# Linear attention and a gated MLP in one kernel: attention in blocks of 64 tokens on four quarters of the array

## The chip, the cores and the metric

One NeuronCore of one Trainium2 chip runs the whole program. The metric is the device time of one execution in microseconds (us), inputs already in HBM. The profile is one execution taken by the hardware profiler. "TensorE" is PE in the rows (PEld: its weight loads), VectorE DVE, ScalarE ACT, GpSimd POOL, SyncE's queue SP.

## The reference

Inputs: q, k, v of 4 sequences x 8 heads x 768 tokens x 64, a decay `lam` per head, MLP weights 512x1536 (gate, value) and 1536x512 (out), a norm weight. All fp32.

```
for each block of 64 tokens:
    intra = (q_b k_b^T * Dmask) v_b            # Dmask[i,j] = lam^(i-j) for i>=j, else 0
    inter = (q_b * lam^(i+1)) kv_state
    out_b = intra + inter
    kv_state = lam^block * kv_state + (k_b * lam^(block-1-j))^T v_b
x   = attention out as 3072 rows of 512
xn  = x / sqrt(mean(x^2) + 1e-6) * rms_g
out = (silu(xn w_gate) * (xn w_val)) w_out
```

The result does not depend on the block's length except for rounding.

## The kernel before

Tokens come in six groups of 512 (`G`), heads in four pairs, so there are 24 pieces of attention, called pairs here (class `Pair`, L457). A pair's q, k, v are loaded in fp32 (`load_qkv`, L92): q and k with the 64 dimensions of two heads along the partitions, k and v again with tokens along them. The attention works in blocks of 128 tokens, four to a group. Its steps per pair, with the lines of their matmuls:

- `scores` (L468, matmul L477): k q^T of each block and head, 64 rows of the array by 128 columns, 128 moving columns; the two heads use the two row halves and write two banks.
- `decay_a` (L489) multiplies them by a mask of powers on VectorE (L497); `decay_k` (L482) scales k on ScalarE; `decay_q` (L499) scales q by the powers `pw` on GpSimd (L501).
- `state_sums` (L503, matmul L510): k^T v of each block, full height by 64 columns, two heads in the two column halves. A sequence's last block needs none.
- `states` (L515): the running state, on VectorE: a copy for a sequence's first block (L523), else state x power + sum (L525).
- `mix_chunks` (L530, matmul L538): masked scores times v; `mix_states` (L543, matmul L549): state times scaled q, 64x64 on the two diagonal quarters, both heads into the one bank `po`. A sequence's first block has no state.
- `keep_output`, `keep_squares` (ScalarE) take the bank away for the norm.

The powers are made in the opening by scans on VectorE (`powers`, L150: 8 masks L153 and 4 rows `pw` L158).

The MLP runs in fp16 with each operand split in a high and a low part, in three products: groups 0 and 1 classically (L668), groups 2 to 5 by a scheme with seven products of quarter blocks (L779); the last layer likewise (L938 for group 0, L1050). Weights are converted from fp32 bits on the chip during groups 0 and 1. Attention of group 0 and part of group 1 fills the opening, before there is an fp16 operand; the rest lies between the MLP's steps.

PSUM has eight banks: four of pool `ps_g` (MLP, and the odd pairs of group 0), two of `ps_s` (scores; for groups 3 to 5 sums and `po` too), two of `ps_o` (`oa`, `ob`: sums and `po` of groups 0 to 2, results of the last layer).

The order of the work on every engine is fixed when the program is built. `Plan` (L1089) holds steps with an engine, a cost, a due time and the tiles that they read, write and open; `Plan.run` (L1154) simulates the engines and takes the steps by due time. `SHIFTS` (L1760) moves single steps' due times. `Plan.shared` (L1150) names the steps of VectorE that GpSimd must not overlap: a GpSimd step after one of them waits for it. `TURN` (L1143) is the planner's charge for going from fp16 work to attention steps and back. Engines then wait on each other by semaphores, each in its own order.

## Time and profile before

| | |
|---|---|
| three timed runs | 630.33, 631.5, 631.6 us; median 631.5 |
| the profiled execution's own time | a span of 628.2 us from its first to its last instruction; what lies around the span is not in the trace |
| TensorE busy | 622.2 us, 99% |
| VectorE, ScalarE, GpSimd busy | 452.8, 383.9, 127.6 us |
| moved by DMA | 144.05 MB, mean 229 GB/s |

Busy time of an engine is the union of its instructions. A matmul's end is modelled: its record lasts longer than the array is taken by it, so spacing of starts, not the length of one, shows what a matmul costs. Rows give the line, engine, operation, output and inputs by the program's names (`pa` scores, `pst` sums, `po` mix), shapes and counts.

### The profile page before, as it was taken

The numbers are of one execution on the slowest core, as the hardware profiler recorded it, in microseconds if no ns is written. First come the engines' busy times: TensorE is split into PE (matmuls) and PEld (weight loads), VectorE is DVE, ScalarE is ACT, GpSimd is POOL, SyncE is SP. The second block draws the span as 40 slices with busy tenths as digits, with TensorE's granted clock in tenths as the row PEclk, the third lists the DMA queues.
The fourth block names the chain that finished last, engine by engine and source line by source line (L and its number), as shares of the span: only waits on it lengthen the run. The fifth ranks groups of instructions, "written<-read, shape, count | busy, mean of one in ns | idle before, by whom it ended". The sixth has DMA issues, their size and how long they took to land.

```text
span 628.2 us, 14174 instructions
## 1 busy us (share of the span) xinstructions
PE 622.2 (99%) x5665; PEld 479.3 (76%) x5665; DVE 452.8 (72%) x886; ACT 383.9 (61%) x724; POOL 127.6 (20%) x113
## 2 busy tenths in 40 slices
PE   9999999999999999999999999999999999999997
PEld 8864444455657777668888888888889888888886
DVE  6889888777787778788875789634874778546641
ACT  3779799986546764568764685534853564445531
POOL 3531201142825665410020110011000110000000
DMA  8899898888646788878878667744675667343401
GB/s 320 305 318 299 313 313 290 288 279 290 231 148 226 258 284 273 275 265 284 269 268 297 216 212 225 244 179 152 226 224 179 202 207 248 109 135 105 148 18 51
DMA packets 56033, 144.05 MB, mean 229 GB/s; under 512 B 5920, under 2 KB 18208, under 8 KB 54560
## 3 DMA queue, kind: packets, MB, share of 16 engines
q1 hardware_dynamic: 55824, 142.64, 67.3%
q8 instruction: 44, 0.72, 0.5%
q10 hardware_dynamic: 144, 0.52, 0.3%
q14 instruction: 21, 0.17, 0.1%
HBM read 106.96 MB, written 36.18 MB: 228 GB/s over the span
## 4 chain that ended last, share of the span: by engine, by line
PE 94%; DMA 2%; DVE 1%; ACT 1%; SPq 0%; issue 0%; POOL 0%; ACTq 0%; POOLq 0%
PE o L1050 20%; PE pa L779 20%; PE pb L779 15%; PE pv L668 9%; PE pg L668 9%; PE o L938 5%; PE pa L477 4%; PE po L538 3%; PE po L549 3%; DMA qkv<-in_qkv_dram 2%; PE o_own L1050 2%; PE pst L510 2%; PE pss L589 1%; PE unread L144 1%; PE pr L630 0%
## 5 line engine op out<-in xcount | busy, mean ns | idle before, releaser
L779 PEld LDWEIGHTS <-gw 128*128 128x128 f16 x1440 | 139.5, 98 | 21.9 <-issue 0.8
L1050 PE MATMUL o<-wo,late 128*128 128x256 f16 x1152 | 143.9, 273 | 0.5 <-ACT late L1061 0.5
L1050 PEld LDWEIGHTS <-late 128*128 128x128 f16 x1260 | 123.0, 98 | 15.1 <-issue 0.8
L668 PEld LDWEIGHTS <-w_half 128*128 128x128 f16 x576 | 53.9, 98 | 60.5 <-issue 1.5
L833 ACT COPY tx<-pa 128x256 f32<-128x256 f32 x96 | 35.3, 371 | 72.9 <-PE pa L779 55.5
L779 PE MATMUL pa<-tx,gw 128*128 128x256 f16 x576 | 77.4, 273 | 0.0
L668 PE MATMUL pv<-x,w_half 128*128 128x512 f16 x288 | 69.2, 379 | 0.2
L668 PE MATMUL pg<-x,w_half 128*128 128x512 f16 x288 | 66.8, 379 | 0.0
L837 DVE TENSOR_TENSOR tx<-pb,tx 128x256 f32<-128x256 f32 x96 | 40.0, 420 | 31.4 <-PE pb L779 29.1
L779 PEld LDWEIGHTS <-gv 128*128 128x128 f16 x576 | 56.0, 98 | 7.4 <-issue 0.2
L501 POOL TENSOR_TENSOR qkv<-qkv,pw 128x512 f32<-128x512 f32 x24 | 30.6, 1275 | 74.8 <-PE pa L477 66.5
L845 DVE TENSOR_TENSOR sg<-pb,sg 128x256 f32<-128x256 f32 x48 | 20.1, 422 | 35.4 <-ACT sg L841 30.7
L1013 DVE TENSOR_TENSOR late<-s,late 128x1024 f16<-128x1024 f32 x30 | 37.3, 1253 | 5.2 <-ACT late L1009 5.1
L708 POOL TENSOR_TENSOR r<-w_half 128x512 f32<-128x512 f16 x24 | 27.7, 1163 | 63.3 <-DVE w_half L440 25.5
L497 DVE TENSOR_TENSOR a<-pa,mask 128x512 f32<-128x512 f32 x48 | 31.4, 683 | 12.0 <-PE pa L477 8.5
L779 PE MATMUL pa<-x,gv 128*128 128x256 f16 x288 | 39.3, 273 | 0.0
L779 PE MATMUL pb<-x,gv 128*128 128x256 f16 x288 | 39.3, 273 | 0.0
L779 PE MATMUL pa<-x,gw 128*128 128x256 f16 x288 | 39.0, 273 | 0.0
L779 PE MATMUL pb<-tx,gw 128*128 128x256 f16 x288 | 39.0, 273 | 0.0
L779 PE MATMUL pb<-x,gw 128*128 128x256 f16 x288 | 38.7, 273 | 0.0
L938 PE MATMUL o<-wo,early 128*128 128x512 f16 x144 | 34.9, 379 | 0.0
L729 POOL TENSOR_TENSOR ws<-ws,ws 128x512 f16<-128x512 f32 x24 | 28.8, 1210 | 29.3 <-DVE en L325 15.3
(152 smaller groups left out, 1031.0 us busy)
## 6 DMA issues: line engine op xcount, KB each, us to landing
gw<-gw_kept SPq DMA_DIRECT2D x48, 640.0 KB, 4.8
qkv<-in_qkv_dram SPq DMA_DIRECT2D x47, 512.0 KB, 6.0
h<-h_kept SPq DMA_DIRECT2D x30, 512.0 KB, 4.1
h_kept<-sg SPq DMA_DIRECT2D x48, 256.0 KB, 3.4
gv<-gw_kept SPq DMA_DIRECT2D x48, 256.0 KB, 4.4
raw_gv<-in_weights_dram SPq DMA_DIRECT2D x11, 1024.0 KB, 7.2
raw_o<-in_weights_dram SPq DMA_DIRECT2D x24, 256.0 KB, 4.4
gw_kept<-ws SPq DMA_DIRECT2D x12, 512.0 KB, 4.2
```

Source lines behind the costliest of these rows:

```text
L477: nc.tensor.matmul(self.pa[j][:, c, :], self.kT[r, c, :], self.qT[r, c, :], start=True, stop=True,)
L497: nc.vector.tensor_mul(self.a[:, j], self.pa[j], decay)
L501: eng.tensor_mul(self.qT, self.qT, pw[:, p : p + 1, :].broadcast_to([P, GC, P]))
L668: nc.tensor.matmul(ps, w[:, kk, :], x[:, kk, :], start=i == kk == 0, stop=i == 2 and kk == NK - 1,)
L708: nc.gpsimd.tensor_add(self.r[:, i], w[:, 0], w[:, 1])
L729: eng.tensor_sub(self.to[:, c, 1], self.t[:, c], self.to[:, c, 0])
L779: nc.tensor.matmul(ps, w(ow, k), x(ox, k), start=first and i == k == 0, stop=i == 2 and k == 1, skip_group_check=True,)
L833: nc.scalar.copy(self.val_sums[:, self.half(t)], self.pa)
L837: nc.vector.tensor_add(v, self.pb, v)
L938: nc.tensor.matmul(self.banks[t], h[:, oh, t * P : (t + 1) * P], wo[:, j, 3 + 2 * k : 5 + 2 * k, ow], start=j == k == i == 0, stop=j == HA ...
L1013: eng.tensor_sub(lo, of, hi)
L1050: nc.tensor.matmul(bank[:, t], ops[:, oh, t * P : (t + 1) * P], w[:, ow], start=n in (1, 2, 5) and q == i == 0 and (t == 0 or bank is own) ...
```

## The change

Attention goes in blocks of 64 tokens, the reference's own. A group is now 256 tokens of two sequences (groups 0 to 2: sequences 0 and 1; 3 to 5: sequences 2 and 3), in place of 512 tokens of one; the host lays out q, k, v so and `send` writes the rows accordingly. Every attention matmul has 64 rows, 64 columns and 64 moving columns, and the loops go round the four 64x64 quarters of the array. Both heads, and both sequences with their heads crossed, lie so that the two row halves write different banks or different partitions.

- Scores: 16 matmuls a pair; sums 16, into the second half of the scores' two banks, so that one buffer `s` of two banks holds both; `decay_a` covers 512 elements a partition in place of 1024.
- States: one step for each of a group's four blocks, with an update for each of the two sequences; a sequence's first state is copied on ScalarE.
- The mix is two halves, `mix_others` and `mix_states` (which begins with the second half of the mix and goes on with the states), 8 + 8 + 16 matmuls. Between them stands a fence: a memset of one column on GpSimd (`between`) that waits for the first half's last matmul, and for which the second half's first matmul waits. Both halves add to the same places from different row halves.
- `po` of groups 0 to 2 and the last layer's results share one buffer `oo` of two banks; `po` of groups 3 to 5 takes the buffer `s`.
- Masks are three scans of 64 a pair on VectorE; all `pw` are made on GpSimd by one copy and six products (`powers_of_pairs`). The row of zeros and its ScalarE instruction (L204, L205) go.
- The planner's costs follow, and the table `SHIFTS` is new: 2726 entries in place of 856.

```diff
-ps_s = ctx.enter_context(tc.tile_pool(name="ps_s", bufs=2, space=PSUM))
+ps_s = ctx.enter_context(tc.tile_pool(name="ps_s", bufs=1, space=PSUM))
...
-lam_b, lam_p, gcol = cs[:, :H], cs[:, H : H + NP], cs[:, H + NP :]
+lam_b, lam_p, gcol = cs[:, :H], cs[:, H : H + 2 * NP], cs[:, H + 2 * NP :]
...
-SLOTS = GC + 1
+LAST = S // D - 1
...
-state = const.tile([P, NP, SLOTS, D], F32, name="state")
-mask = const.tile([P, H, P], F32, name="mask")
-pw = const.tile([P, NP, P], F32, name="pw")
-def powers(p, part):
-    if part < 2:
-        h = 2 * p + part
-        nc.vector.tensor_tensor_scan(
-            mask[:, h, :], lam_b[:, h : h + 1].broadcast_to([P, P]), ident, 0.0,
-            ALU.mult, ALU.add,
+state = const.tile([P, NP, 2, 2, D], F32, name="state")
+mask = const.tile([P, NP, 3, D], F32, name="mask")
+pw = const.tile([P, NP, 2, 1, D], F32, name="pw")
+diag = const.tile([P, D], F32, name="diag")
+nc.gpsimd.tensor_add(diag, ident[:, :D], ident[:, D:])
+def powers(p, n):
+    h = 2 * p + n % 2
+    nc.vector.tensor_tensor_scan(
+        mask[:, p, n], lam_b[:, h : h + 1].broadcast_to([P, D]), diag, 0.0, ALU.mult, ALU.add,
+    )
+def powers_of_pairs():
+    to = pw.rearrange("p n q o i -> p (n q) (o i)")
+    lam = lam_p.rearrange("p (n i) -> p n i", i=1)
+    nc.gpsimd.tensor_copy(to[:, :, :1], lam)
+    n = 1
+    while n < D:
+        nc.gpsimd.tensor_mul(
+            to[:, :, n : 2 * n], to[:, :, :n],
+            to[:, :, n - 1 : n].broadcast_to([P, 2 * NP, n]),
         )
-    else:
-        nc.vector.tensor_tensor_scan(
-            pw[:, p, :], lam_p[:, p : p + 1].broadcast_to([P, P]), zeros, 1.0,
-            ALU.mult, ALU.add,
-        )
+        n *= 2
...
+fence = const.tile([P, 1], F32, name="fence")
+def after(instruction, name, reason="row tiles"):
+    tc.add_manual_dep(
+        instruction, name,
+        mybir.DependencyInfo(mybir.DependencyClass.Sync, mybir.DependencyReason.DATA), reason=reason,
+    )
...
-        self.scores_room, self.scores_tag = (ps_g, "g") if self.turn else (ps_s, "s")
+        self.scores_tag = "g" if self.turn else "s"
+        self.mix_tag = "oo" if self.early else "s"
     qT, kT, k, v = (property(lambda s, i=i: loaded[s.m, s.p][i]) for i in range(4))
-    def scores(self, chunks=range(GC)):
+    def block(self, c, s):
+        return (self.m % 3) * GC + (c % 2) * 2 + s, c // 2
+    def scores(self):
         m, p = self.m, self.p
-        if 0 in chunks:
-            self.pa = [
-                self.scores_room.tile([P, GC, P], F32, tag=self.scores_tag, name=f"pa_{m}_{p}_{j}")
-                for j in range(2)
+        if self.turn:
+            self.pa = None
+            self.banks = [
+                ps_g.tile([P, G], F32, tag="g", name=f"pa_{m}_{p}_{j}") for j in range(2)
             ]
-        for c in chunks:
-            for j, r in enumerate(heads):
-                nc.tensor.matmul(
-                    self.pa[j][:, c, :], self.kT[r, c, :], self.qT[r, c, :],
-                    start=True, stop=True,
-                )
+        else:
+            self.pa = ps_s.tile([P, 2, G], F32, tag="s", name=f"pa_{m}_{p}")
+            self.banks = [self.pa[:, j] for j in range(2)]
+        for c, q, s, row in itertools.product(range(2), repeat=4):
+            b, half, r = 2 * q + c, slice(s * D, (s + 1) * D), heads[row]
+            nc.tensor.matmul(
+                self.scored(row)[half, c, q], self.kT[r, b, half], self.qT[r, b, half],
+                start=True, stop=True, skip_group_check=True,
+            )
+    def scored(self, row):
+        return self.banks[row][:, : GC * D].rearrange("p (c q i) -> p c q i", c=2, q=2)
...
     def decay_a(self, part=None):
         p = self.p
         if not part:
-            self.a = att.tile([P, 2, GC, P], F32, tag="a", name=f"a_{self.m}_{p}")
-        for j in range(2):
-            if part in (None, j):
-                h = 2 * p + j
-                decay = mask[:, h : h + 1, :].broadcast_to([P, GC, P])
-                nc.vector.tensor_mul(self.a[:, j], self.pa[j], decay)
+            a = att.tile([P, (2 * GC + 2 * (GC - 1)) * D], F32, tag="a", name=f"a_{self.m}_{p}")
+            self.a = a[:, : 2 * GC * D].rearrange("p (r c x) -> p r c x", r=2, c=2)
+            self.inner = a[:, 2 * GC * D :].rearrange("p (q t d) -> p q t d", q=2, d=D)
+        for row in range(2) if part is None else (part,):
+            decay = mask[:, p : p + 1, row : row + 2].rearrange("p n q i -> p n (q i)")
+            nc.vector.tensor_mul(
+                self.a[:, row], self.scored(row).rearrange("p c q i -> p c (q i)"),
+                decay.broadcast_to([P, 2, 2 * D]),
+            )
     def decay_q(self, eng=nc.gpsimd):
+        q = self.qT.rearrange("p (q c) (s i) -> p q (c s) i", q=2, s=2)
+        eng.tensor_mul(q, q, pw[:, self.p].broadcast_to([P, 2, GC, D]))
+    def sum_of(self, c, s):
+        return self.banks[s][:, (GC + c) * D : (GC + c + 1) * D]
+    def state_sums(self):
+        for c in range(GC):
+            for s in range(2):
+                t, q = self.block(c, s)
+                if t == LAST:
+                    continue
+                half = slice(s * D, (s + 1) * D)
+                for j, r in enumerate(heads):
+                    nc.tensor.matmul(
+                        self.sum_of(c, s)[heads[j ^ q]], self.k[half, c, r], self.v[half, c, r],
+                        start=True, stop=True, skip_group_check=True,
+                    )
+    def state(self, t):
+        if t % GC == GC - 1:
+            return state[:, self.p, :, t // GC % 2]
+        return self.inner[:, :, t % GC]
+    def first_states(self):
+        sums = self.banks[0][:, GC * D : 2 * GC * D].rearrange("p (q x) -> p q x", q=2)
+        nc.scalar.copy(self.state(0), sums[:, :, :D])
+    def states(self, t):
         p = self.p
-        eng.tensor_mul(self.qT, self.qT, pw[:, p : p + 1, :].broadcast_to([P, GC, P]))
-    def state_sums(self):
-        m, p = self.m, self.p
-        pool, tag = (ps_o, "oa") if self.early else (ps_s, "s")
-        self.pst = pool.tile([P, GC, P], F32, tag=tag, name=f"pst_{m}_{p}")[:, :, :D]
-        for c in range(GC):
-            if (m * GC + c) % SEQ_CH < SEQ_CH - 1:
-                for r in heads:
-                    nc.tensor.matmul(
-                        self.pst[r, c, :], self.k[:, c, r], self.v[:, c, r],
-                        start=True, stop=True,
-                    )
-    def states(self, chunks=range(GC)):
-        m, p = self.m, self.p
-        for c in chunks:
-            g = m * GC + c
-            if g % SEQ_CH == SEQ_CH - 1:
-                continue
-            new = state[:, p, g % SLOTS, :]
-            if g % SEQ_CH == 0:
-                nc.vector.tensor_copy(new, self.pst[:, c, :])
-            else:
+        for c, s in [(c, s) for s in range(2) for c in range(GC)]:
+            at, q = self.block(c, s)
+            if at == t:
+                new, old = (self.state(x)[:, q] for x in (t, t - 1))
                 nc.vector.scalar_tensor_tensor(
-                    new, state[:, p, (g - 1) % SLOTS, :], pw[:, p, P - 1 : P],
-                    self.pst[:, c, :], ALU.mult, ALU.add,
+                    new, old, pw[:, p, q, 0, D - 1 : D], self.sum_of(c, s), ALU.mult, ALU.add,
                 )
-    def mix_chunks(self, chunks=range(GC)):
-        m, p = self.m, self.p
-        if 0 in chunks:
-            pool, tag = (ps_g, "g") if self.turn else (ps_o, "ob") if self.early else (ps_s, "s")
-            self.po = pool.tile([P, GC, P], F32, tag=tag, name=f"po_{m}_{p}")
-        po = self.po
-        for c in chunks:
-            for j, r in enumerate(heads):
+    def mix(self, other):
+        for c, q, j in itertools.product(range(2), repeat=3):
+            s = j ^ q ^ other
+            half = slice(s * D, (s + 1) * D)
+            a = self.a[half, j ^ q, c, q * D : (q + 1) * D]
+            nc.tensor.matmul(
+                self.po[heads[j], q, 2 * c + s], self.v[half, 2 * q + c, heads[j]], a,
+                start=bool(other) and c == 0, stop=False, skip_group_check=True,
+            )
+            if not (other or c or q or j):
+                after(traced[-1], self.fence)
+        self.last = traced[-1].name
+    def mix_others(self):
+        pool = ps_o if self.early else ps_s
+        po = pool.tile([P, 2, G], F32, tag=self.mix_tag, name=f"po_{self.m}_{self.p}")
+        self.po = po[:, :, : GC * D].rearrange("p q (b i) -> p q b i", b=GC)
+        self.mix(1)
+    def between(self):
+        nc.gpsimd.memset(fence, 0.0)
+        after(traced[-1], self.last)
+        self.fence = traced[-1].name
+    def mix_states(self):
+        self.mix(0)
+        for b, q, j in itertools.product(range(GC), range(2), range(2)):
+            t = self.m % 3 * GC + b
+            if t:
+                r = heads[j ^ q]
                 nc.tensor.matmul(
-                    po[r, c, :], self.v[:, c, r], self.a[:, j, c, :],
-                    start=c == 0, stop=False, skip_group_check=True,
+                    self.po[heads[j], q, b], self.state(t - 1)[r, q],
+                    self.qT[r, 2 * q + b // 2, b % 2 * D : (b % 2 + 1) * D],
+                    start=False, stop=True, skip_group_check=True,
                 )
-    def mix_states(self):
-        m, p, po = self.m, self.p, self.po
-        for c in range(GC):
-            g = m * GC + c
-            if g % SEQ_CH:
-                for r in heads:
-                    nc.tensor.matmul(
-                        po[r, c, :], state[r, p, (g - 1) % SLOTS, :], self.qT[r, c, :],
-                        start=False, stop=True, skip_group_check=True,
-                    )
...
-    TURN = {"scores": 0.1, "mix_chunks": 0.05, "mix_states": 0.0, "state_sums": 0.0}
+    TURN = dict.fromkeys(("scores", "mix_others", "mix_states", "state_sums"), 0.1)
...
-        return eng == "POOL" or eng == "DVE" and fn.__name__ in self.SHARED
+        return eng == "POOL" and fn.__name__ != "between" or eng == "DVE" and fn.__name__ in self.SHARED
...
 def pair_scores(q, at):
     n = f"{q.m}_{q.p}"
-    for i in range(2):
-        step("PE", 0.545, at + 0.02 * i, q.scores, range(2 * i, 2 * i + 2), r=[f"q{n}:q", f"q{n}:K"],
-             w=[f"pa{n}_0", f"pa{n}_1", "turn:pa"],
-             new=[] if i else [(f"pa{n}_{j}", q.scores_tag) for j in range(2)])
+    room = [(f"pa{n}{j}", "g") for j in "ab"] if q.turn else [(f"pa{n}", "s")]
+    names = [name for name, _ in room]
+    step("PE", 0.47, at, q.scores, r=[f"q{n}:q", f"q{n}:K"], w=[*(f"{x}:p" for x in names), "turn:pa"], new=room)
     for j in range(2):
-        step("ACT", 0.5, at + 0.1, q.decay_k, j, r=[f"mask{2 * q.p + j}"], w=[f"q{n}:k"])
-    for j in range(2):
-        step("DVE", 0.65, at - 1, q.decay_a, j, r=[f"pa{n}_{j}", f"mask{2 * q.p + j}"], w=[f"a{n}"], new=[] if j else [(f"a{n}", "a")])
+        step("ACT", 0.5, at + 0.1, q.decay_k, j, r=[f"mask{q.p}"], w=[f"q{n}:k"])
+    masks = [f"mask{q.p}"]
+    if q.turn:
+        for j in range(2):
+            step("DVE", 0.42, at - 1, q.decay_a, j, r=[f"{names[j]}:p", *masks], w=[f"{names[j]}:s", f"a{n}", f"a{n}:i"], new=[] if j else [(f"a{n}", "a")])
+    else:
+        step("DVE", 0.82, at - 1, q.decay_a, r=[f"{names[0]}:p", *masks], w=[f"{names[0]}:s", f"a{n}", f"a{n}:i"], new=[(f"a{n}", "a")])
     step("POOL", 1.27, at + 0.1, q.decay_q, r=[f"pw{q.p}"], w=[f"q{n}:q"])
 def pair_sums(q, at):
     n = f"{q.m}_{q.p}"
-    step("PE", 0.5, at, q.state_sums, r=[f"q{n}:k", f"q{n}:v"], w=[f"pst{n}", "turn:pst"],
-         new=[(f"pst{n}", "oa" if q.early else "s")])
-    for i in range(2):
-        step("DVE", 0.58, at - 1, q.states, range(2 * i, 2 * i + 2), r=[f"pst{n}", f"pw{q.p}"], w=[f"state{q.p}"])
+    sums = [f"pa{n}{j}:s" for j in "ab"] if q.turn else [f"pa{n}:s"]
+    step("PE", 0.47, at, q.state_sums, r=[f"q{n}:k", f"q{n}:v"], w=[*sums, "turn:pst"])
+    for t in range(q.m % 3 * GC, min(q.m % 3 * GC + GC, LAST)):
+        if t:
+            step("DVE", 0.58, at - 1, q.states, t, r=[*sums, f"pw{q.p}"], w=[f"state{q.p}", f"a{n}:i"])
+        else:
+            step("ACT", 0.32, at - 1, q.first_states, r=sums, w=[f"state{q.p}", f"a{n}:i"])
 def pair_mix(q, at):
     n = f"{q.m}_{q.p}"
     m, p = q.m, q.p
-    for i in range(2):
-        step("PE", 0.49, at + 0.01 * i, q.mix_chunks, range(2 * i, 2 * i + 2), r=[f"q{n}:v", f"a{n}"],
-             w=[f"po{n}", "turn:po"],
-             new=[] if i else [(f"po{n}", "g" if q.turn else "ob" if q.early else "s")] + [(f"x{m}", f"xs{SLOT_OF[m]}")] * (p == 0))
-    step("PE", 0.8, at + 0.05, q.mix_states, r=[f"q{n}:q", f"state{p}"], w=[f"po{n}"])
+    step("PE", 0.25, at, q.mix_others, r=[f"q{n}:v", f"a{n}"], w=[f"po{n}", "turn:po"],
+         new=[(f"po{n}", q.mix_tag)] + [(f"x{m}", f"xs{SLOT_OF[m]}")] * (p == 0))
+    step("POOL", 0.1, at + 0.05, q.between, w=[f"po{n}"])
+    step("PE", 0.75, at + 0.05, q.mix_states, r=[f"q{n}:v", f"a{n}", f"q{n}:q", f"state{p}", f"a{n}:i"], w=[f"po{n}"])
...
-        for part in range(3):
-            w = f"pw{p}" if part == 2 else f"mask{2 * p + part}"
-            step("DVE", 0.38, -3.2 + 0.4 * p + 0.15 * (part == 2), powers, p, part, r=["cs"] + ["wv11"] * (part == 2), w=[w])
+        for n in range(3):
+            step("DVE", 0.33, -3.2 + 0.4 * p + 0.1 * n, powers, p, n, r=["cs"], w=[f"mask{p}"])
+    step("POOL", 2.2, -3.2, powers_of_pairs, r=["cs"], w=[f"pw{p}" for p in range(NP)])
...
 SHIFTS = {
-    14: 13.03, 16: 14.75, 17: 15.55, 18: 16.43, 19: 19.96, 20: 21.25, 21: 18.22, 22: 18.97,
...
+    0: -18.489, 1: -18.389, 2: -16.832, 3: -14.132, 4: -13.834, 5: -11.949, 6: -9.369, 7: -6.301,
...
 }
```

## Rows read from the trace of the kernel before

**Rows 1.** The page: busy time by engine, then the chain by engine.

```profile
PE 622.2 (99%) x5665; PEld 479.3 (76%) x5665; DVE 452.8 (72%) x886; ACT 383.9 (61%) x724; POOL 127.6 (20%) x113
...
PE 94%; DMA 2%; DVE 1%; ACT 1%; SPq 0%; issue 0%; POOL 0%; ACTq 0%; POOLq 0%
```

**Rows 2.** Busy time by stage (start:end, length, each engine, clock, DMA share, GB/s).

```profile
6.00:34.00 28.00, 27.47 (x417) 23.50 (x416) 23.94 (x65) 18.50 (x38) 14.35 (x12) 1.00 0.90 343
34.00:430.00 396.00, 395.27 (x3441) 276.78 (x3440) 306.84 (x601) 268.90 (x499) 107.02 (x88) 1.00 0.78 260
...
31.00:100.00 69.00, 68.74 (x449) 35.37 (x446) 60.59 (x119) 59.28 (x114) 13.59 (x11) 1.00 0.90 306
```

**Rows 3.** Instructions by line: the four attention lines of TensorE.

```profile
L477 PE MATMUL pa<-qkv 64*128 64x128 f32 x384 | 29.1, 287 | 0.0
L538 PE MATMUL po<-a,qkv 128*64 128x128 f32 x384 | 26.5, 278 | 0.0
L549 PE MATMUL po<-qkv,state 64*64 64x128 f32 x320 | 22.5, 276 | 0.0
L510 PE MATMUL pst<-qkv 128*64 128x64 f32 x320 | 13.9, 228 | 0.0
```

**Rows 4.** TensorE timeline around single visits (start, busy time, instructions merged).

```profile
256.79 0.71 PE L779 MATMUL pb<-x,gw 128*128 128x256 f16 x5
257.43 1.16 PE L477 MATMUL pa<-qkv 64*128 64x128 f32 x16
258.52 0.72 PE L779 MATMUL pb<-x,gv 128*128 128x256 f16 x5
...
267.77 0.71 PE L477 MATMUL pa<-qkv 64*128 64x128 f32 x8
...
313.96 0.57 PE L510 MATMUL pst<-qkv 128*64 128x64 f32 x12
...
380.70 0.92 PE L510 MATMUL pst<-qkv 128*64 128x64 f32 x24
```

**Rows 5.** TensorE timeline: first stretch, a visit of two pairs, last stretch.

```profile
6.09 1.16 PE L477 MATMUL pa<-qkv 64*128 64x128 f32 x16
...
403.27 1.10 PE L538 MATMUL po<-a,qkv 128*64 128x128 f32 x16
404.30 1.09 PE L549 MATMUL po<-qkv,state 64*64 64x128 f32 x16
405.32 1.09 PE L538 MATMUL po<-a,qkv 128*64 128x128 f32 x16
...
428.95 1.09 PE L549 MATMUL po<-qkv,state 64*64 64x128 f32 x16
```

**Rows 6.** Instructions by line: VectorE for scores, states and powers; 256 elements from PSUM.

```profile
L497 DVE TENSOR_TENSOR a<-pa,mask 128x512 f32<-128x512 f32 x48 | 31.4, 683 | 12.0 <-PE pa L477 8.5 <-PE po L538 2.9
L525 DVE SCALAR_TENSOR_TENSOR state<-state,pw,pst 128x64 f32<-128x64 f32 x64 | 17.6, 279 | 4.3 <-PE pst L510 2.7
L523 DVE COPY state<-pst 128x64 f32<-128x64 f32 x16 | 3.5, 217 | 2.4 <-PE pst L510 2.0
L837 DVE TENSOR_TENSOR tx<-pb,tx 128x256 f32<-128x256 f32 x96 | 40.0, 420 | 31.4 <-PE pb L779 29.1 <-ACT tx L833 1.9
L158 DVE TENSOR_TENSOR_SCAN pw<-cs,w_half 128x128 f32<-128x128 f32 x4 | 1.6, 397 | 0.0
```

**Rows 7.** Instructions by line: GpSimd, decay_q and a small memset.

```profile
L501 POOL TENSOR_TENSOR qkv<-qkv,pw 128x512 f32<-128x512 f32 x24 | 30.6, 1275 | 74.8 <-PE pa L477 66.5 <-DVE w_half L440 4.3 <-DVE pw L158 2.8
L133 POOL MEMSET power<- 128x4 f32 x1 | 0.1, 102 | 0.0
```

**Rows 8.** Timeline of the opening: last mix of group 0, first gate; lift of weight 0.

```profile
23.41 0.87 PE L549 MATMUL po<-qkv,state 64*64 64x128 f32 x12
33.73 1.04 PE L668 MATMUL pg<-x,w_half 128*128 128x512 f16 x4
...
19.75 1.15 ACT L209 ACTIVATE w<-w_half 128x1024 f32<-128x1024 f32 x1
```

More of the change, by code (lines that the diff above doesn't have):

```diff
@@ L931, in product @@
         def product(self, j, k, t):
[L932 to L935 removed]
+            if j == k == t == self.i == 0:
+                plain[self.m] = ps_o.tile([P, 2, 2, HG], F32, tag="oo", name=f"o_{self.m}")
+            self.banks[t] = plain[self.m][:, t]
             h = early[0][:, j, ((1, 0), (2, 3))[k][self.i]]
@@ L1029, in product @@
             if q == 0 and 0 in tokens and n in (1, 2, 5):
-                bank = ps_o.tile(
-                    [P, 2, HG], F32, tag="oa" if a else "ob", name=f"o_{self.m}_{n}"
-                )
-                if a:
-                    self.a = bank
-                else:
-                    self.b = bank
+                if n == 1:
+                    both = ps_o.tile([P, 2, 2, HG], F32, tag="oo", name=f"o_{self.m}")
+                    self.a, self.b = both[:, 0], both[:, 1]
                 if self.m == NG - 1 and n != 2:
@@ L1370, in plain_rows_steps @@
             r = PlainRows(m, i)
-            banks = [f"op{m}_{i}_{t}" for t in range(2)]
+            banks = [f"op{m}:{t}" for t in range(2)]
             for j in range(HALF):
@@ L1374, in plain_rows_steps @@
                     for t in range(2):
-                        new = [] if j or k else [(banks[t], "oa" if t == 0 else "ob")]
+                        new = [] if i or j or k or t else [(f"op{m}", "oo")]
                         step("PE", 0.655, at + length * (i * 12 + 2 * j + k + 0.5 * t) / 24, r.product, j, k, t,
@@ L1959, in retention_swiglu_kernel @@
         now, gaps = 1.5, True
-        traced, ahead = nc.cur_bb.bb.instructions, None
+        ahead = None
         for t, i in order:
@@ L2018, in _consts @@
     rows = _np.broadcast_to(lam, (P, lam.shape[-1]))
-    halves = _np.repeat(lam.reshape(-1, 2).T, P // 2, axis=0)
+    pairs = _np.stack([lam.reshape(-1, 2), lam.reshape(-1, 2)[:, ::-1]], axis=1)
+    halves = _np.repeat(pairs.reshape(-1, 2).T, P // 2, axis=0)
     return _np.ascontiguousarray(_np.concatenate([rows, halves, rms_g.reshape(-1, P).T], axis=1))
```

43 lines of the change are left out of this document (19 added, 24 removed), and 493 rows, old and new, of the table SHIFTS.

## Prediction

> **What bounds the kernel now.** I read the page's busy shares and chain first. TensorE is busy for 622.2 of 628.2 us, the other engines 72% or less, and 94% of the chain that ended last is TensorE [rows 1]. [...] A microsecond taken off TensorE after 34 us is therefore a microsecond of the span, until another engine runs full. The nearest is VectorE: 60.6 of 69.0 us between 31 and 100 us, 23.9 of 28.0 in the opening [rows 2]. The third view, instructions by line, has the attention's four TensorE lines: 29.1 + 26.5 + 22.5 + 13.9 = 92.0 us [rows 3]. The last, the timeline, prices them. Each fp32 matmul shows as two instructions.
>
> **Price of one attention matmul.** 16 instructions of scores are busy for 1.16 us and 8 for 0.71: 56 ns each. 24 of the sums take 0.92 and 12 take 0.57: 29 ns each [rows 4]. [...] A visit, a stretch of attention between two stretches of fp16 work, costs more than its rounds: the matmuls before it take 0.64 us for five where five at 109 ns take 0.545 (0.095 on entry); and 12 sums occupy 0.50 us, that is 0.57 less the 0.07 by which busy time runs past the next start (1.16 against 257.43 to 258.52), where six rounds need 0.35 (0.15 more) [rows 4]. So 0.245 us a visit.
>
> **Before.** The timeline has 97 stretches of attention lines in 42 visits, the first at 6.09, the last ending with the one at 428.95 [rows 5]. 92.0 - 97 x 0.07 + 42 x 0.095 = 89.2 us of TensorE.
>
> **After.** A pair has 16 matmuls of scores, 16 of mix, 16 of sums and 16 with states, less four sums in 8 pairs and four states in 8: 2 x (24 x 64 - 64) = 2944 instructions, all 64x64 quarters with N = 64. No row has four quarters at once. Bounds: 14.5 ns an instruction (four in a round of 58) and 29 ns (two): 42.7 or 85.4 us. I take 14.5, because each pairing in it stands in a row: scores put two row halves side by side, mix and sums two column halves, and neither costs a round more than its columns [rows 4, 5].
>
> The mix and the states send both row halves into one PSUM bank. Line 549 does so already, the diagonal quarters into one bank: 16 in 1.02 us, where line 538, full height, takes 1.03 for as many [rows 5]. [...]
>
> Visits: at best 42, as now; at worst 96, four steps a pair with fp16 work between all. The fence forces work between the two halves of a mix, so I take 60: 14.7 us (10.3 to 23.5). TensorE then spends 42.7 + 14.7 = 57.4 us on attention: 31.8 less (23.0 to 36.2).
>
> **What of it reaches the end.** 27 of the 97 stretches lie before the first gate at 33.73 [rows 5, 8], so 8.9 us of the 31.8 fall in the opening and 22.9 behind it, where TensorE sets the pace: these I count whole.
>
> In the opening VectorE is the limit. Per pair decay_a goes from 2 x 683 ns to about 840 (512 elements for 1024, so between 683 and 1366; the nearest row, 256 elements from PSUM on line 837, has 420, and two of it are 840). States go, in a sequence's first third, from three updates and a copy (1.04 us) to six updates (1.65; 275 ns each busy) with the copy on ScalarE; in the second from 0.77 to eight (2.20); in the last from 0.83 to 1.65 [rows 6]. So +0.1 us for each of group 0's four pairs and +0.9 for each of three pairs of group 1. The four scans of pw leave (-1.6); the masks become twelve of half the length for eight: between -0.8 and +1.6, I take +0.3. Sum +1.8: 23.9 + 1.8 = 25.7 us of VectorE in a stretch of 28.0 [rows 2], so the opening shortens by 2.3 at most; by 0 if its chain is elsewhere. First gates need group 0's norm, whose last mix starts at 23.41, and weight 0, which ScalarE begins to lift only at 19.75 [rows 8]. I take 2.
>
> The powers on GpSimd, one copy and six products of 512 elements in all, lie between 0.7 us (seven at 102 ns) and 2.0 (seven with one of 1275 among them) [rows 7], in a queue that has nothing else before the first decay_q. I count nothing; if the first scores are there sooner than the powers, pair 0's second half comes up to 2 us late, and the opening's gain is gone.
>
> Over the kernel VectorE gains 24 x (0.84 - 1.31) = -11 for decay_a and 160 x 0.275 - 17.6 - 3.5 = +23 for states [rows 6], net +12 (+10 after the powers). Behind the opening this lies beside TensorE, 77% full on average; between 31 and 100 us it rises to some 62.6 in 66. Bounds 0 and 5 us, I take 1.
>
> The fence: 24 memsets, 102 ns each [rows 7]. TensorE's queue stops at the first matmul of the second half until the memset has run, with all fp16 work behind it; the memset queues on GpSimd behind operations of up to 1275 ns. An fp16 step of 12 matmuls (1.3 us) between covers it. Where the cover fails, up to 0.6 us each: 0 to 14 us, I take 1. Scores and sums now hold both banks of one buffer until the states are formed, and a late pair's mix takes the same two; with twelve late pairs in the 240 us up to the last row of [rows 5] I count nothing, and a pair that waits shows as late scores.
>
> Sum: -22.9 - 2 + 1 + 1 = -22.9. 628.2 - 22.9 = 605.3 us of span. The runs' median, 631.5, is 3.3 above the profiled span, so 608.6.
>
> **Rivals.**
> 1. VectorE or the fence takes over, behind the opening: the saving shrinks by the upper bounds, 5 and some 10 us, and the opening gains nothing: -22.9 + 15 = -7.9, 623.6. For: VectorE's 88% between 31 and 100, and GpSimd's long operations. Against: fp16 steps lie everywhere between. Result 616 to 627, as much of either comes. Chance 0.26.
> 2. Slower: four quarters do not stream together. If only two do, 85.4 + 14.7 + 2 = 102.1 against 89.2: about 644. It decides once an instruction takes more than (89.2 - 14.7 - 2)/2944 = 24.6 ns, a round of four 98 ns. For: nothing in the rows is issued faster than one in 29 ns on average [rows 4]. [...] Chance 0.07.
> 3. A floor per matmul, whatever its tile. If instructions cannot follow one another in under some 25 ns, the 2944 take 73.6 us, and the time is 628.2 - 0.9 + 2 + 3.3 = 632.6, no gain. 29 ns in rows 4 neither shows nor excludes it. Chance 0.05. [...]
> 4. The change does not do what it says, as when the fence makes the two halves follow each other without cover and every visit costs double: 60 x 0.245 more, 623, in the range of rival 1. Chance 0.02.
> 5. Two row halves wait for each other at one bank: mix and states go two at a time, 1472 x 14.5 ns = 21.3 us more, about 630. Against it stands line 549's pace [rows 5]. Chance 0.02.
>
> **The numbers.** The forecast, 599 to 616, has 0.58. The range 598 to 627 adds rivals 1 and 4 (0.86 together) and leaves out some of either edge. Its low end is 42 visits with most of the opening's gain; the high end 96 visits with rival 1's losses. 0.2%, about 1.3 us, is what a measurement of this kernel can tell from no change. Faster 0.87: forecast, rivals 1, 4 and half of 5. Same 0.03: part of rival 3. Slower 0.10: rival 2, the rest of 3 and edges.
>
> **What would show it.** Right: 32 scores in about 0.5 to 0.6 us, 24 to 32 sums likewise; the attention's four lines busy for some 60 us in place of 92.0; TensorE still over 98% after the opening; first gate about 32. Wrong: scores still over 0.9 us a pair (rival 2) or 0.8 (rival 3); idle TensorE put down to GpSimd's memset or to VectorE's states (rival 1); a granted clock under 1.00, which no row hints at.

## The result: 1.4% slower

Five runs after the change have a median of 639.67 us (637.6 to 645.41) beside 631.6 us (630.33 to 633.34) for five of the kernel before on the same chip: a ratio of 1.014, interval 1.0096 to 1.0183. The forecast was 608.6, and the range, 598 to 627, does not hold the result. The profiled execution is the longest of the five (645.41 us, span 643.6), so what is read from its trace below adds up to a loss of 15.4 us, where the medians differ by 8.1. The five spread over 7.8 us: a few us between two single traces, as in where the first gate lies, need not be the work of an edit.

The page after the change, busy time by engine, the granted clock in 40 slices, and the queue that brings the engines their instructions:

```profile
PE 616.6 (96%) x7263; PEld 470.2 (73%) x7263; DVE 456.6 (71%) x966; ACT 384.6 (60%) x731; POOL 131.0 (20%) x145
...
PEclk9879999999999999999999999999999999999999
...
q8 instruction: 57, 0.93, 0.6%
```

TensorE had 622.2 busy in 628.2 us [rows 1]; now 27 us are idle. The instructions by line (shapes kept apart) say that this is not because attention costs more: its lines are busy for 76.9 us, for the 92.0 of [rows 3].

```profile
L582 PE MATMUL po<-a,qkv 64*64 64x64 f32 x768 | 23.2, 237 | 4.2 <-issue 2.4 <-ACT sq L631 1.1 <-ACT x L620 0.3
L508 PE MATMUL pa<-qkv 64*64 64x64 f32 x768 | 17.8, 234 | 0.9 <-DVE ws L777 0.6 <-PE pa L551 0.3
L551 PE MATMUL pa<-qkv 64*64 64x64 f32 x704 | 17.2, 233 | 0.3 <-ACT junk L420 0.3
L607 PE MATMUL po<-qkv,a 64*64 64x64 f32 x576 | 13.8, 226 | 2.7 <-issue 2.7
L607 PE MATMUL po<-qkv,state 64*64 64x64 f32 x128 | 4.9, 224 | 0.0
```

**The opening.** The first gate (the first fp16 product of the MLP, `pg`) comes at 46.00 us; it came at 33.73 [rows 8]. The table by stage (columns as in [rows 2]):

```profile
6.00:12.00 6.00, 6.00 (x152) 5.35 (x155) 3.37 (x15) 1.98 (x5) 3.14 (x9) 1.00 1.01 392
12.00:20.00 8.00, 5.03 (x190) 4.52 (x185) 3.85 (x16) 2.14 (x5) 3.08 (x4) 0.87 0.74 267
20.00:31.00 11.00, 7.61 (x268) 6.62 (x261) 6.93 (x22) 7.12 (x16) 4.73 (x6) 0.94 0.90 291
31.00:60.00 29.00, 26.06 (x500) 19.28 (x503) 22.18 (x62) 19.15 (x39) 10.07 (x12) 0.82 0.68 228
60.00:100.00 40.00, 38.61 (x260) 18.61 (x251) 33.37 (x66) 34.17 (x64) 9.22 (x8) 1.00 0.81 275
```

No engine is full there: VectorE, which I took for the limit, has 14.2 of 25 us between 6 and 31. The timeline of TensorE shows where time stands still:

```profile
12.75 0.69 PE L508 MATMUL pa<-qkv 64*64 64x64 f32 x32 [0.30 <-PE pa L551]
13.23 0.28 PE L582 MATMUL po<-a,qkv 64*64 64x64 f32 x2
15.87 0.40 PE L582 MATMUL po<-a,qkv 64*64 64x64 f32 x11 [2.36 <-issue]
...
28.10 0.44 PE L607 MATMUL po<-qkv,a 64*64 64x64 f32 x16
31.23 0.34 PE L607 MATMUL po<-qkv,a 64*64 64x64 f32 x8 [2.69 <-issue]
...
33.94 1.13 PE L508 MATMUL pa<-qkv 64*64 64x64 f32 x32
...
46.00 1.04 PE L727 MATMUL pg<-x,w_half 128*128 128x512 f16 x4
```

Two stops of 2.36 and 2.69 us lie in the middle of a loop that waits for no operand ("issue"). Counting the instructions of TensorE's queue from the start (matmuls, weight loads and the queue's own waits), they come after the 449th and the 1217th, which are 3 x 256 apart; and the trace's DMA records have a packet of 16 KB on the instruction queue beginning at 13.29 and at 28.59 us, which ends 1.5 us before TensorE goes on. My reading: TensorE had run out of instructions. After the stops the granted clock falls, to 0.50 from 17.92 to 21.33 us and from 31.57 to 41.81: 32 scores that took 0.69 us at 12.75 take 1.13 at 33.94.

**Behind the opening.** From the first gate to the end it is 597.6 us, where it was 594.5. The waits of TensorE (total, times, longest):

```profile
PE o L1106 <- DVE late L1125: 3.7, 6, 0.9
PE po L607 <- issue: 2.7, 1, 2.7
PE po L582 <- issue: 2.4, 1, 2.4
PE o L1106 <- ACT late L1117: 2.2, 4, 0.8
PE pg L727 <- ACT w_half L440: 1.8, 2, 0.9
...
PE pa L838 <- DMA gw<-gw_kept: 1.2, 1, 1.2
...
PE po L582 <- POOL fence L597: 0.3, 1, 0.3
```

L1106 is the last layer, whose two banks now are one tile. A timeline of all engines shows how it waits: ScalarE takes bank a away from 515.25 to 515.94, and the next product, into bank b, starts only then.

```profile
513.09 2.13 PE L1106 MATMUL o<-wo,late 128*128 128x256 f16 x18
...
515.25 0.69 ACT L1117 ACTIVATE late<-o,ik 128x512 f32<-128x512 f32 x1 [0.59 <-PE o L1106]
...
515.99 1.25 PE L1106 MATMUL o<-wo,late 128*128 128x256 f16 x10 [0.78 <-ACT late L1117]
```

To see where the stretch behind the first gate goes, I added up the time from each matmul's start to the next one's, by what it belongs to (a wait counts for the matmul before it). e1, e7 and e13 are runs of the next section:

| us behind the first gate | before | after | e1 | e7 | e13 |
|---|---|---|---|---|---|
| attention (1028 matmuls, then 2128) | 62.1 | 42.5 | 42.6 | 42.5 | 43.3 |
| last layer | 173.5 | 182.8 | 176.0 | 175.7 | 173.2 |
| first layer | 348.0 | 356.7 | 353.9 | 351.7 | 351.8 |
| norms, fillers, rest | 10.8 | 15.6 | 15.4 | 11.9 | 11.2 |
| together | 594.5 | 597.6 | 588.0 | 581.8 | 579.4 |

So attention gives back 19.6 us behind the gate, and the work around it takes 22.7 more. Of the first layer's 8.7, some 5 are idle TensorE before its products (5.4 us, for 0.2 before the change), the longest parts behind ScalarE's `w_half` (1.8) and loads of `gw` (1.2 at once); the rest of it I cannot assign. The last layer's 9.3 go with the tile: the kernels that keep the merged tile and the table (`after`, e2, e3) have 181.9 to 183.2 us there, those with two tiles (e1, e4 to e9, e12 to e14) 171.1 to 177.5.

### The profile page after: what moved, and what is told of

Its sections match the earlier page's. It is cut to its first block, busy times and chain, and to the rows that moved or that the text cites. A ratio compares the mean times of both kernels' runs of the same rounds, so it can differ in the third digit from the quotient of the medians.

```text
span 643.6 us, 17543 instructions
## 1 busy us (share of the span) xinstructions
PE 616.6 (96%) x7263; PEld 470.2 (73%) x7263; DVE 456.6 (71%) x966; ACT 384.6 (60%) x731; POOL 131.0 (20%) x145
## 5 line engine op out<-in xcount | busy, mean ns | idle before, releaser
L1106 PE MATMUL o<-wo,late 128*128 128x256 f16 x1152 | 145.4, 273 | 6.0 <-DVE late L1125 3.7
L1106 PEld LDWEIGHTS <-late 128*128 128x128 f16 x1260 | 122.1, 98 | 22.8 <-issue 7.9
L900 ACT COPY sg<-pa 128x256 f32<-128x256 f32 x48 | 17.8, 372 | 30.4 <-PE pa L838 28.8
L1069 ACT CAST late<-s 128x1024 f16<-128x1024 f32 x30 | 31.3, 1046 | 5.9 <-DVE s L1053 3.2
```

The lines of the kernel that those rows point to most:

```text
L900: nc.scalar.copy(self.sg[:, self.half(1)], self.pa)
L1069: nc.scalar.copy(hi, of)
L1106: nc.tensor.matmul(bank[:, t], ops[:, oh, t * P : (t + 1) * P], w[:, ow], start=n in (1, 2, 5) and q == i == 0 and (t == 0 or bank is own) ...
```

## The experiments

The theory: (a) the merged tile makes each bank wait for the other's eviction; (b) TensorE gets its instructions in blocks of 256, quarters use up a block before the next is there; (c) what follows in the opening adds to it: the granted clock of 0.50, late loads, and fillers, which are matmuls whose result nobody reads, put in where the plan has TensorE idle. Rivals: the quarters or the fence themselves, or the new table.

**e1 to e4: undo single parts.** e1 makes two tiles of the merged one again (also for the early pairs' `po`, whose eviction becomes two instructions); the order stays.

```diff
-both = ps_o.tile([P, 2, 2, HG], F32, tag="oo", name=f"o_{self.m}")
-self.a, self.b = both[:, 0], both[:, 1]
+self.a, self.b = (
+    ps_o.tile([P, 2, HG], F32, tag=f"o{b}", name=f"o{b}_{self.m}") for b in "ab"
+)
```

> The changed kernel, its order of work untouched, with the last layer's two result banks as two tiles again in place of one tile of two banks (groups 0 to 2 take their mix away in two instructions of 256 elements for that). Theory A (one tile for both banks couples them: a product into one bank waits for the eviction of the other): the waits of the last layer's products on VectorE's line 1125, ScalarE's line 1117 and ScalarE's row evictions, 3.7 + 2.2 + 0.8 us of idle TensorE in the changed kernel, go, and it is 4 to 8 us faster, about 633 to 636. Rival B (the evictions are late because VectorE and ScalarE are full): the waits stay with other names and the time stays within 2 us.

Measured: 639.33 us, ratio 1.0106 (1.0065 to 1.0147). The waits are gone: TensorE's products of the last layer stood still for 3.7 + 2.2 us in `after` (the 7.9 us of "issue" are its weight loads, idle at the same moments), and for none of these in e1. The last layer is 6.8 us shorter, the stretch behind the first gate 9.6 us (table). But the median does not show the gain: the first gate came at 49.51, behind a stop of 4.1 us at 45.78. The last layer by its line, first of `after`, then of e1 (us, times), and that stop:

```profile
  issue: 7.9, 11
  DVE late L1125: 3.7, 6
  ACT late L1117: 2.2, 4
```

```profile
  issue: 0.3, 1
...
PE poa L613 <- issue: 4.1, 1, 4.1
```

e2 issues the load of weight 0, which in `after` is issued at 5.27 us and so lies ahead of the first instruction packet (13.29), only behind pair 1's `decay_k`:

```diff
-load_gv(0)
...
+if (self.m, self.p, half) == (0, 1, 1):
+    behind, begun = traced[-1].name, len(traced)
+    load_gv(0)
+    for x in traced[begun:]:
+        after(x, behind, "late load")
```

> The changed kernel with the load of weight 0 issued only after pair 1's k is scaled, at about 10.5 us in place of 5.3, so that it does not lie in the DMA queues between 6 and 13 us. Theory A (TensorE's 2.4 us without work at 13.3 us is its instruction fetch, which waits behind loads in full DMA queues): the first fetch comes within about 1.5 us of its need, the idle time at 13.3 falls under 1 us, the first gate comes at 42 to 44 us in place of 46.0, the granted clock in the opening rises, and the time falls by 2 to 5 us. Rival B (that wait is the fence, or the states): it stays at about 2.4 us, and the time is unchanged within 1.5 us.

Measured: 641.58, ratio 1.0155 (1.0125 to 1.0185). The first gate is at 41.78, but the first stop stays (2.1 us) and the median is no lower: a miss. e3 makes the fillers 512 columns wide and a quarter as many:

```diff
-for _ in range(n):
-    nc.tensor.matmul(ps[:, :P], ident, ident, start=True, stop=True)
...
+for _ in range((n + GC - 1) // GC):
+    nc.tensor.matmul(ps.rearrange("p (o c) -> p o c", o=GC), ident, wide, start=True, stop=True)
```

> The changed kernel with the opening's unread filler matmuls four times as wide and a quarter as many: the same array time, some 130 TensorE instructions fewer before 46 us. Theory A (instruction fetch): the two waits of 2.4 and 2.7 us fall to other places in the program and become shorter, as fetches are wanted later; 1 to 5 us faster. Rival B (fence or states set these waits): the waits stay where they are in the work, time within 1.5 us.

Measured: 640.07, ratio 1.0137 (1.0098 to 1.0177), first gate 42.70: no gain either. e4 has all three.

> The three edits together. Theory A: the gains add up, 8 to 15 us under the changed kernel, 624 to 631, and the granted clock stays at 1.00 through most of the opening. Rival C (the new priority table is what costs, an order that the chip does not follow): less than 5 us gained, waits of another kind in their place.

Measured: 633.09, ratio 1.0016 (0.9994 to 1.0037): 6.6 us less than `after`, equal to before. From first gate to end it takes 584.4 us, 10.1 less than before, but the gate is at 46.80: what the quarters save behind the opening is lost in it. Its timeline has the longest stop of all, after the 705th instruction, 256 behind the 449th:

```profile
18.60 0.65 PE L558 MATMUL pa<-qkv 64*64 64x64 f32 x26
23.36 0.48 PE L558 MATMUL pa<-qkv 64*64 64x64 f32 x6 [4.12 <-issue]
```

**e5: the stops by themselves.** e4 with two bursts of quarter matmuls that wait for nothing:

```diff
...
+for i in range(512):
+    a, b = i // 2 % 2 * D, i % 2 * D
+    nc.tensor.matmul(
+        ps[a // D][b:b + D, :D], ident[a:a + D, b:b + D], ident[a:a + D, a:a + D],
+        start=True, stop=True, skip_group_check=True,
+    )
```

> The kernel of e4_all_three with two bursts added, each of 512 matmuls of 64x64 on the four quarters (1024 TensorE instructions with their weight loads) that wait for nothing and whose results nobody reads: one at about 100 us, where loads fill the DMA engines to 0.85, one behind the last product, where DMA is quiet. Theory (the stalls of the opening are TensorE waiting for its own instructions): at 14.5 ns a matmul a burst would be 7.4 us, but every 128 matmuls (256 instructions) it stops until the next 16 KB of the instruction queue have come: stalls of 2 to 4 us at 100 us, of about 1 us at the quiet end, so 12 to 18 us and 8 to 11 us. Rival (the stalls were waits for operands or banks that the trace doesn't show): both bursts run through in 7.4 us.

Measured: 686.23 us. Each matmul of this fp32 identity was issued twice, so a burst has 1024, twice what I had reckoned with. The timeline, from the quiet end:

```profile
659.34 2.10 PE L152 MATMUL burst<-ident 64*64 64x64 f32 x128 [0.89 <-issue]
663.09 2.10 PE L152 MATMUL burst<-ident 64*64 64x64 f32 x128 [1.65 <-issue]
666.56 2.10 PE L152 MATMUL burst<-ident 64*64 64x64 f32 x128 [1.38 <-issue]
670.30 2.10 PE L152 MATMUL burst<-ident 64*64 64x64 f32 x128 [1.65 <-issue]
674.32 2.10 PE L152 MATMUL burst<-ident 64*64 64x64 f32 x128 [1.92 <-issue]
678.07 2.10 PE L152 MATMUL burst<-ident 64*64 64x64 f32 x128 [1.65 <-issue]
```

This shows (b). Without any wait TensorE stops after exactly 128 matmuls with their 128 weight loads, each time. And in all the kernels here, every stop of over 1 us that is put down to "issue" lies after the 449th instruction or a multiple of 256 behind it, whatever work stands there: after the 705th in e4 and e7, the 961st in e13, the 1729th in e1 and e3, the 16833rd at 659.34 us above. Within a block the matmuls run at about 15 ns, but a block takes 3.5 to 4.0 us, so 27 to 31 ns a matmul in the long run. The burst at 113 us tells that the block, and not the array, sets this pace:

```profile
118.81 2.99 PE L152 MATMUL burst<-ident 64*64 64x64 f32 x128 [2.00 <-issue]
122.53 5.92 PE L152 MATMUL burst<-ident 64*64 64x64 f32 x256 [0.74 <-issue]
129.72 0.50 PE L152 MATMUL burst<-ident 64*64 64x64 f32 x17 [1.26 <-issue]
```

From 122 to 126 us the granted clock was 0.50 (0.87 on average from 113 to 140), and 128 matmuls took longer; the stop behind them shrank to 0.04 us (126.26), and the blocks still began 3.5 to 3.7 us apart. Its other stops are of 0.7 to 2.0 us, no longer than at the end; but DMA had fallen to 0.15 of its time in it (113 to 140 us; 0.03 at the end), so it does not tell what loads add.

**e6 and e7: what the stops and fillers do to the opening.** `after` puts 917 matmuls ahead of the first gate, before had 435; attention of group 1 is among them. e6 is e4 with group 1's attention 8 us later in the order of every engine:

```diff
...
+def key(t, i):
+    q = getattr(plan.steps[i][3], "__self__", None)
+    return t + (8 if isinstance(q, Pair) and q.m == 1 else 0)
+order = plan.resequence(order, key)
```

> The kernel of e4_all_three with all attention steps of group 1 put 8 us later in the order on every engine, nothing else. Theory (what lengthens the opening is that 900 instead of 430 matmuls are put ahead of the first gate, so that instruction fetches fall into group 0's chain): the first gate moves from 46.8 us to 38 to 42, the whole time falls by 2 to 6 us, to 627 to 631. Rival (group 0's own chain and its loads set the gate): first gate 45 or later, the time within 1 us of e4_all_three's 633.1, or longer, because group 1's attention now lies between products.

Measured: 664.67, ratio 1.0525 (1.0507 to 1.0543). The gate is where the theory had it, at 40.34 us with 645 matmuls ahead of it; the time is not, and for two reasons that the theory had left out. The moved times let in fillers: 96 over the kernel where e4 has 32, and behind the gate they take 25.9 us from start to start, for 2.9 in e4, so that not only the order differs. And in the waits of the SP queue between 20 and 64 us the loads stand behind buffers that group 1 now holds longer, the weights behind them, and DMA falls to 0.49 of its time (stage 31 to 60). The time therefore does not tell where group 1 belongs:

```profile
SPq L96 <- PE pob L620: 17.4, 3, 13.5
```

```profile
31.00:60.00 29.00, 20.39 (x389) 12.40 (x388) 14.90 (x42) 14.13 (x33) 7.51 (x8) 0.95 0.49 168
```

e7 is e4 without the fillers behind the first 6 us:

```diff
-if gaps and idle > 0.8:
+if gaps and idle > 0.8 and now < 5:
```

> The kernel of e4_all_three without the filler matmuls behind the first 6 us. Theory (the fillers are put in where the plan has TensorE idle, but run also when TensorE is late, so they add to the delay): first gate 2 to 5 us earlier than 46.8, whole time 628 to 631. Rival (the fillers only fill waits, and hold the granted clock up): without them the clock shows half rate between 10 and 45 us, first gate not earlier than 46, time 634 to 640.

Measured: 630.87, ratio 0.999 (0.9966 to 1.0014); gate 44.75. Both were half right: 2.2 us less than e4, a difference that the two intervals leave within the noise, and the clock does fall (0.79 between 12 and 20, 0.63 between 20 and 31 us), where e4 had 1.00 and 0.69. Fillers cost about what they hold up.

**e8 and e9: do loads delay the instructions?** In e7 the second block came only with a packet that began at 19.99 us, in the midst of loads issued from 15.05 on. e8 is e7, e9 is e4, with group 1's loads behind the sums of group 0's last pair:

```diff
...
+if m == 1:
+    for x in traced[-2:]:
+        after(x, held[0], "late load")
```

> The kernel of e7_no_fillers with one more wait: the loads of group 1's q, k, v are issued behind the sums of group 0's last pair (about 20 us) instead of from 15.05 us on. Theory (a fetch of TensorE's instructions queues behind the loads issued before it, which is why the second fetch of the opening came 5 us late in e7): the packet of that fetch starts at about 16 instead of 19.99 us, the stop of 2.0 us at 20.4 us goes or shrinks under 1 us, the first gate comes 2 to 4 us earlier (41 to 43 us), and the time falls by as much, to 627 to 629. Rival (the fetch is slow whatever the loads do, and group 1's attention now waits for its data): the stop stays, scores of group 1 begin later than 27 us, the time is 631 or more.

> The kernel of e4_all_three (with its fillers) with the same wait for the loads of group 1. Theory: the stop of 4.3 us at 19.0 us goes or shrinks under 1.5 us, first gate 43 to 44 instead of 46.8, time 629 to 631 against e4's 633.1; the granted clock of 20 to 31 us, 0.69 in e4, is back above 0.9, as the drop followed that stop. Rival: the stop stays, time 633 or more.

Measured: e8 633.02 (1.0021, 0.9997 to 1.0045), e9 634.13 (1.0031, 1.0006 to 1.0055). In e8 the packet begins at 18.26 and the stop at 20.4 us is gone, in e9 the stop of 4.1 us shrinks to 1.4 and the clock between 20 and 31 us is back at 1.00. From TensorE's going on after the first stop to the start of the next packet it takes 5.3 us in e7 and 5.4 in e4, and 2.2 and 2.5 with the loads held: loads do delay the blocks. The first gates stay, at 45.20 and 46.24, and so do the times: group 1 now waits for its data (1.2 us in each), the time went from one wait into another. In e9, e4 and e5 one more stop, of 1.8 us at 45 to 46 us, stands right before the gate; the waits put it down to ScalarE, but it lies after the 1729th instruction, 1.5 us behind the end of a 16 KB packet, as the others do. In e2 a stop of 2.2 us after the 961st is put down to VectorE in the same way.

**e10 and e11: the table.** Both kernels with `SHIFTS = {}`:

> The kernel after the change with its table of priorities emptied, so that the steps lie by their plain due times. Theory (the order matters on both sides, and the table is not what costs the change its gain): both kernels without tables are 5 to 10 per cent slower than with them, and this one is faster than e11_before_no_table by up to 10 us, since attention takes less of TensorE. Rival (the new table is the fault): this kernel is no slower than 640 us, or gains 20 us or more on e11.

> The kernel before the change with its table of priorities emptied. Expected with the theory of e10: 660 to 700 us. Rival: near 632 us, its table would then be worth nothing.

Measured: 697.76 and 691.33 us, one run each. Without tables both lose some 9%, of which fillers behind the gate are some 30 us in each (31.7 and 30.0); the change is the slower one by about as much as with them, so the new table does not look like the fault. But the change is not the faster one without tables either; there my theory missed.

**e12 to e14: another order.** If (a) to (c) are the causes, an order chosen with these prices should win some back. The planner's order is kept and 914 steps are moved, by trying moves and keeping those that shorten a sum of step costs with the prices of e1 to e8 in it.

```diff
+MOVES = {
...
+}
 order = plan.run()
+order = plan.resequence(order, MOVES)
```

> The kernel of e7_no_fillers in another order: the planner's order is taken, and 914 of its 2726 steps are moved so that the sum of step costs comes out 6 us shorter when TensorE is given what the runs showed and the planner does not know: two tiles for the result banks, no fillers, 256 instructions at a time with the next ones 3.6 us (6 to 7 before 20 us) after the last were begun, and attention at half rate between 14 and 40 us. Theory (the losses of the opening and of the tail are of the order, and the order was made without these prices): first gate 41 to 44 us, time 624 to 628, faster than e7 and than the kernel before (631.7). Rival (the order is as good as it gets, or such prices don't carry over to the chip): 630 or more.

Measured: 871.88. The moved times let in 590 fillers, 257.7 us of TensorE: a mistake that says nothing of the order.

> e12 again without the 590 filler matmuls (257.7 us in its trace) that the moved times had let in by mistake: the ten at the start are left and no others, so against e7_no_fillers only the order differs. Theory (what is left of the loss lies in an order made without the prices that the runs showed): first gate 41 to 44 us, time 624 to 628, below e7's 630.9 and the 631.6 of the kernel before. Rival (the order is as good as it gets, or prices summed step by step don't carry over to the chip): 630 or more.

> e13 with only those 89 moves whose steps lie in the first 50 us. Theory: the first gate as early as in e13 (41 to 44 us), the time between e13 and e7, 626 to 630. Rival: the gate stays at 44 to 47 us, as in all kernels that keep group 1's attention ahead of it; time 630 or more.

Measured: e13 622.82 us (621.36 to 624.53), ratio 0.9857 (0.9837 to 0.9878), a little better than expected; e14 629.82, 0.9977 (0.9961 to 0.9993). e13 beats both kernels: 8.4 us less than before, 16.9 less than `after`, with the quarters, the fence and every attention matmul as the change has them. This shows that the quarters do not forbid a gain; that the gain comes from the prices and not from any new search it does not show, as the kernel before was not searched again. Its gate is at 43.32; TensorE behind it (stages of e13):

```profile
20.00:31.00 11.00, 7.34 (x220) 6.86 (x212) 7.06 (x27) 6.57 (x17) 3.96 (x5) 0.66 0.68 235
31.00:60.00 29.00, 26.09 (x551) 17.95 (x552) 24.20 (x63) 21.20 (x48) 11.22 (x13) 0.86 0.79 272
60.00:100.00 40.00, 40.00 (x205) 19.22 (x204) 36.21 (x72) 35.94 (x71) 6.82 (x6) 1.00 0.89 296
100.00:300.00 200.00, 198.79 (x2258) 126.85 (x2257) 159.66 (x356) 142.34 (x272) 80.41 (x72) 1.00 0.81 274
300.00:600.00 300.00, 299.56 (x3434) 263.55 (x3432) 210.00 (x408) 166.91 (x325) 23.65 (x24) 1.00 0.61 198
```

From 60 us on it is full, as the kernel before was; the opening still has stops (one of 3.1 us in its waits) and a granted clock of 0.66 between 20 and 31 us, and the gate is 9.6 us later than before. So most of the opening's loss is not in the order that I found. e14, with the moves of the first 50 us alone, has the earlier gate (42.08) but not the time: the moves behind it are worth 7.0 us.

## Why the prediction was wrong, by its steps

- **Price of an attention matmul, 14.5 ns: right.** That the 29 ns of [rows 4] are two instructions at once, 58 ns a round, no row shows, but the starts in that trace do: two sums start 6 to 7 ns apart, the next two 51 to 53 ns behind, and two scores come every 112 ns, as does one instruction of 128 fp32 columns on the whole array (`pr`, L626). In the trace after the change four quarters start within 20 ns and the next four 58 to 59 ns behind the first, in most rounds beyond 60 us. An isolated visit of 32 scores takes 0.62 us from its start to that of the next work (lines below), 0.48 of it from its first matmul's start to its last's; within a block e5 has 14.8 ns a matmul; 2944 matmuls as counted. The sign of "some 60 us" for the four lines was not met all the same (76.9 busy): records of neighbouring lines overlap, and part of the opening ran at a granted clock of 0.50. Rivals 2, 3 and 5 fell: four quarters stream, also in the mix (L582), whose two row halves write one bank (the same 58 to 59 ns for four), and the 14.8 ns lie below rival 3's 25, which is about what products of one column take in the trace before (`pc`, L314: starts 25 to 26 ns apart). But rows 4 never had 128 matmuls in a row: in the long run e5 has 27 to 31 ns, the pace of rival 3, for another reason.

```profile
51.47 0.69 PE L508 MATMUL pa<-qkv 64*64 64x64 f32 x32
52.09 1.04 PE L727 MATMUL pg<-x,w_half 128*128 128x512 f16 x4
```

- **Visits, 60 at 0.245 us: nearly.** There are 70, of which 59 behind the gate take 42.5 - 2128 x 0.0145 = 11.6 us, 0.20 each.
- **"22.9 behind it, where TensorE sets the pace: these I count whole": failed.** Attention behind the gate did fall, by 19.6 us. TensorE had set the pace there (395.27 of 396.00 us busy at a clock of 1.00 [rows 2]), but only while nobody made it wait; the change made it wait, and the other work on it took 22.7 us more, so that the term of -22.9 came out as +3.1 in the trace.
- **PSUM, "I count nothing": failed.** I counted pairs that wait for a buffer, and gave the shared `oo` no price at all. The last layer became 9.3 us longer; two tiles give 6.8 of it back (table, e1). The front had said that `po` and the last layer share one buffer of two banks; what I missed is that with both banks in one tile a product into one waits for the eviction of the other (3.7 + 2.2 us in `after`, nothing in e1).
- **"In the opening VectorE is the limit ... I take 2": failed.** In the trace it is 12.3 us longer. VectorE was not full, and had not been (TensorE was busy 27.47 of the 28 us of that stage, VectorE 23.94 [rows 2]); shorter matmuls ran TensorE into blocks that were not there, with stops of 5.1 us in the traced run, a clock of 0.82 between 31 and 60 us, fillers (90 for 28 over the kernel) and loads issued later (16.85 for 11.78 us). Of these, e7 prices the fillers net of the clock at 2.2 us, within the noise; e8 shows that a stop taken away is not yet a gate that comes sooner; how much each of the others holds I can't say.
- **"A granted clock under 1.00, which no row hints at": it came, for a cause outside the rows.** It fell to 0.50 at 17.92 and 31.57 us, 2.1 and 0.3 us after the two stops had ended.
- **The fence, 1 us: right in size**, 0.3 us once. VectorE, +1: most of the idle TensorE put down to it is the merged tile's (3.7 us), not the states'; rival 1 named the wrong waits.

The slower side had 0.10, nearly all of it for quarters that would not stream (rival 2) or for a floor under each matmul (rival 3). Rival 3 did charge per instruction instead of per column, but as a pace inside a stretch; none of it was for a supply of instructions that runs out.

## What to carry to other kernels

When a change replaces few long instructions by many short ones, count instructions per microsecond as well as columns: here a block of 256 had to last about 3.7 us (3.5 to 4.0 in e5), longer under loads (5.3 us to the next packet in e7, 2.2 with the loads held in e8), and a dense run of quarters uses it up in half of that (128 matmuls at 14.8 ns, 1.9 us). Two accumulators whose evictions should overlap belong in two tiles, even if their banks lie side by side: in e1 that made the last layer 6.8 us shorter. And an order tuned to one set of prices must be chosen again when the prices change: e7 and e13 differ in the order alone, 630.9 and 622.8 us (whether the old order had such a reserve too is open).

## What was not expected of the hardware, and what stays open

- In e5, with DMA quiet, TensorE stops after every 256 instructions (0.9 to 1.9 us), and a block takes 3.5 to 4.0 us, at a granted clock of 0.50 (3.7 us at 122.53) as at 1.00. In the opening, with loads under way, the next block took longer: 4.12 us of standstill in e4, 1.4 when loads were held back (e9).
- Matmuls on four quarters start 15 ns apart on average within a block (e5). The products of one column in the kernel before (`pc`) start 25 to 26 ns apart.
- Open: why the gate stays at 42 to 47 us (49.51 in e1) with group 1's attention ahead of it, whatever single wait is taken away. The supply of instructions alone accounts for part, by an estimate: the 917 matmuls ahead of the gate in `after` are with their loads 1834 instructions, 5.4 blocks beyond the 449th, which at e5's 3.5 to 4.0 us take 19 to 22 us from 15.87 on, to 35 or 38 us; the kernel before had 435 matmuls there. Open too is whether a search like that of e13 would shorten the kernel before as well, whose TensorE was 99% busy: it was not tried. Nor was taking the fence away, which keeps two additions to the same place apart.
